# Top-k attention with a maxout MLP: one batch's scores kept in DRAM, the last batch in two halves, masks without sums

## The chip, the cores and the metric

The kernel runs on one core of one Trainium2 chip. The core has five engines with instruction queues of their own: PE (matrix products; PEld is its weight load), DVE (vector work on SBUF and PSUM), ACT (one function over a tile, with scale, bias and a sum), POOL (vector work on SBUF only) and SP (here it only issues DMAs). Each runs its queue in order and waits on semaphores for the others. The metric is the device time of one execution in microseconds (us).

## The reference

```python
def _attn_ref(q, k, v):                       # q, k, v: (8, 8, 576, 64) float32
    scores = scale * np.matmul(q, k.transpose(0, 1, 3, 2))
    kth = np.partition(scores, -32, axis=-1)[..., -32:-31]
    scores = np.where(scores >= kth, scores, -1000000000.0)
    scores = scores - np.max(scores, axis=-1, keepdims=True)
    attn = np.exp(scores)
    attn = attn / (np.sum(attn, axis=-1, keepdims=True) + 1e-09)
    return np.matmul(attn, v)

def _moe_ref(x, w1, w2, w3, w_out):           # x: (4608, 512), w: (512, 768), w_out: (768, 512)
    h = np.maximum(np.maximum(x @ w1, x @ w2), x @ w3)
    return h @ w_out
```

Attention keeps the 32 largest of 576 scores in each row. Its output, all heads side by side, goes through an MLP that takes the largest of three products.

## The kernel before

**Units.** A batch has 8 heads, taken as 4 pairs. A unit is (batch, pair, quarter): 128 queries against all 576 keys for both heads of a pair, so a score tile of 128 x 2 x 576. The last 64 queries of two pairs make one mixed unit. There are 18 units in a batch and 144 in all; `units` lists them, and its order is the order of ranks.

**A unit's steps.** `qk` makes the scores on PE. For the first batch (`whole`) and for all mixed units it takes the float32 inputs as they are, 4 or 8 matmuls; for the rest `prep` has cut queries and keys into a high and a low part (an ACT cast, a POOL subtraction), and 12 matmuls add three products. There is one PSUM tile for scores. `evac` (ACT) copies and scales them into one of five score tiles `ssb` in SBUF. `sweep` (DVE) takes the eight largest of each seventh of a row into `L`. `negate` (POOL) and `pivot` (DVE, five pieces p1 to p5) work out a pivot `Q[0]` that lies between the 24th and the 32nd largest: p1 takes the eight largest of the lower halves of `L`, p2 and p3 work on the negated upper halves, p4 joins them. `sign` (ACT) writes the sign of pivot minus score and sums it, which counts the scores above the pivot. `window` (POOL) multiplies scores and signs, `below` (DVE) takes the eight largest under the pivot, and `place`, `leave`, `pick` choose the 32nd by the count. `mask` (DVE) pushes the scores under it away and also sums how many they are. `expo` (ACT), `denominator`, `inverse`, `widen`, `turn` (PE transposes), `turned` (ACT), `values` (PE) and `scaled_x` end in the batch's attention output.

**MLP.** `mlp` runs a batch's MLP in float16 products of high and low parts, in two passes of 256 and 320 tokens (the first batch in three spans). It needs the attention output of all pairs for its tokens and the weights, which DVE decodes (`decode`) and ACT and PE cut into two halves (`cut`) in the first 200 us.

**Review.** `review` compares the counts of a batch's masks with the values kept in `Q` and `kth`. If a row was not settled, a flag starts a loop at the end that does all batches again in a plain way.

**Order.** Nothing is left to the hardware: `in_order` takes all steps as pieces with an engine, a cost, needs and rings of buffers, and writes the queues. Each engine takes the piece of lowest rank that can start soon enough; ranks are the unit's number plus an offset for the kind of step (`OFFSETS`). The MLP's pieces are in `fill`: PE takes them when nothing else can start. Queues run as written, so a late piece holds up all that stands behind it.

Of the kernel before, what the change touches and what calls it, by code (L numbers as in the profile page):

```python
# [27 lines left out]
FULL = 1  # L28
PMB = 2
# [3 lines left out]
STICK = 59.0  # L33
WINDOW = 150
LEAD = 69.6
LOCK_A = -150.0
LOCK_B = -100.0
OFFSETS = {'E0': -9.14, 'E1': -5.65, 'E2': 1.85, 'N': -40.3, 'T0': 2.84, 'T1': 9.84, 'T2': 3.75, 'Y': -2.73, 'Z':
# [33 lines left out]
def in_order(pieces, fill):  # L72
# [34 lines left out]
    left = len(pieces) + len(fill)  # L107
    while left:
        best = None
        low = min((q[0].rank for q in queues.values() if q), default=0.0)  # L110
# [12 lines left out]
        (fills if fills[x.engine][:1] == [x] else queues)[x.engine].remove(x)  # L123
# [1052 lines left out]
```

## Time and profile before

| | |
|---|---|
| median of 3 runs | 1194.25 us (1192.98 to 1196.03) |
| profiled execution, device time | 1193.76 us |
| its span | 1192.0 us |
| PE busy | 1132.5 us (95%) |
| DVE busy | 1098.2 us (92%) |
| ACT busy | 1023.2 us (86%) |
| POOL busy | 825.2 us (69%) |
| mean DMA traffic | 46 GB/s |

The span is the time from the first to the last instruction that the profiler saw. An engine is busy while an instruction of it runs; waiting, branching and issuing DMAs are not counted. PE's matmuls overlap in its pipeline and their ends are modelled, so the distance from one start to the next tells more of PE than a busy time.

### The profile page before, as it was taken

How to read it: one execution, taken by the hardware profiler on the slowest of the kernel's cores; microseconds unless marked ns; L12 is line 12 of the kernel's file. 1: busy time of each engine (PE TensorE's matmuls, PEld its weight loads, DVE VectorE, ACT ScalarE, POOL GpSimd, SP SyncE). 2: the span in 40 equal slices, each digit the busy share in tenths (PEclk: the TensorE clock that was granted, in tenths of full speed). 3: DMA queues.
4: the chain of work that ended last, by engine and by line, in shares of the span. 5: the costliest groups of instructions: out<-in, count | busy, mean ns of one | idle time of the engine just before them, and what ended most of it. 6: DMA issues, size and time to landing. Idle time of an engine off the chain costs nothing.

```text
span 1192.0 us, 30104 instructions
## 1 busy us (share of the span) xinstructions
PE 1132.5 (95%) x9699; PEld 814.3 (68%) x9699; DVE 1098.2 (92%) x5543; ACT 1023.2 (86%) x2390; POOL 825.2 (69%) x1277
## 2 busy tenths in 40 slices
PE   5668889999999999999999999999999999999997
PEld 2344557878777767676777768676777768676864
DVE  6999999999999999999999999999999999999611
ACT  3878999999989898999988989899999999899621
POOL 2454776778778867778777878777877877877410
PEclk8789989999999999999999999999999999999999
DMA  8521111001110022002110021002100021000000
GB/s 290 209 86 38 59 34 62 2 28 61 38 43 10 1 88 61 19 2 70 41 40 10 2 87 61 19 2 70 60 21 11 1 88 32 19 2 10 10 18 30
DMA packets 28677, 54.70 MB, mean 46 GB/s; under 512 B 7776, under 2 KB 7776, under 8 KB 28512
## 3 DMA queue, kind: packets, MB, share of 16 engines
q1 hardware_dynamic: 28512, 52.71, 13.3%
q8 instruction: 78, 1.28, 0.5%
q14 instruction: 87, 0.71, 0.2%
HBM read 43.25 MB, written 9.44 MB: 44 GB/s over the span
## 4 chain that ended last, share of the span: by engine, by line
PE 64%; DVE 24%; ACT 6%; POOL 3%; issue 2%; DMA 1%; SPq 0%; ACTq 0%; DVEq 0%; POOLq 0%
PE m L766 28%; PE tr L709 9%; PE tr L678 8%; PE s L511 7%; PE m L826 6%; DVE L L528 6%; DVE Q L581 5%; DVE ssb L622 5%; PE s L503 2%; ACT w L567 2%; POOL w L575 2%; ACT pm L632 1%; DVE h L775 1%; PE tr L673 1%; DVE nR L552 1%
## 5 line engine op out<-in xcount | busy, mean ns | idle before, releaser
L575 POOL TENSOR_TENSOR w<-ssb,w 128x576 f32<-128x576 f32 x288 | 407.2, 1422 | 145.2 <-ACT w L567 54.9
L766 PE MATMUL m<-xh,wall 128*128 128x256 f16 (+3 forms) x2448 | 439.0, 279 | 4.1 <-ACT wall L336 3.5
L766 PEld LDWEIGHTS <-wall 128*128 128x128 f16 x3672 | 347.6, 98 | 82.6 <-issue 13.3
L766 PE MATMUL m<-xl,wall 128*128 128x256 f16 (+3 forms) x1224 | 339.1, 279 | 0.0
L528 DVE MAX8 L<-ssb 128x8 f32<-128x82 f32 (+1 forms) x2016 | 315.8, 228 | 1.8 <-ACT ssb L519 1.7
L632 ACT ACTIVATE pm<-ssb,nb 128x576 f32<-128x576 f32 x288 | 224.2, 779 | 25.5 <-DVE ssb L622 20.6
L622 DVE SCALAR_TENSOR_TENSOR ssb<-ssb,kth 128x576 f32<-128x576 f32 x288 | 238.4, 839 | 0.2
L567 ACT ACTIVATE w<-ssb,Q 128x576 f32<-128x576 f32 x288 | 222.3, 775 | 14.0 <-DVE Q L560 12.9
L690 ACT COPY pT<-tr 128x512 f32<-128x512 f32 (+1 forms) x432 | 215.8, 512 | 20.7 <-PE tr L675 9.9
L581 DVE MAX8 Q<-w 128x8 f32<-128x576 f32 x288 | 215.9, 750 | 5.1 <-POOL w L575 4.3
L678 PE MATMUL tr<-ident,pm 128*128 128x128 f32 x1152 | 178.7, 281 | 12.8 <-ACT pm L632 9.1
L519 ACT ACTIVATE ssb<-s 128x1152 f32<-128x1152 f32 x144 | 163.6, 1136 | 20.3 <-PE s L503 18.9
L709 PE MATMUL tr<-pT,vt 128*64 128x256 f32 (+2 forms) x2000 | 177.6, 327 | 1.0 <-ACT pT L690 1.0
L678 PEld LDWEIGHTS tr<-ident,pm 128*128 128x128 f32 x1152 | 130.2, 142 | 54.8 <-ACT pm L632 20.3
L709 PEld LDWEIGHTS tr<-pT,vt 128*64 128x64 f32 x2000 | 111.2, 138 | 61.9 <-issue 21.5
L775 DVE SCALAR_TENSOR_TENSOR h<-m,rises,h 128x256 f32<-128x256 f32 (+3 forms) x204 | 99.8, 489 | 45.4 <-PE m L766 42.7
L826 PE MATMUL m<-wall,hh 128*128 128x512 f16 x432 | 128.6, 379 | 0.0
L781 POOL TENSOR_TENSOR hl<-h,hh 128x256 f16<-128x256 f32 (+3 forms) x102 | 83.2, 816 | 61.7 <-ACT hh L778 61.0
L511 PE MATMUL s<-kT,qT 64*128 64x288 f32 x1344 | 118.6, 308 | 0.9 <-ACT ssb L519 0.8
L511 PEld LDWEIGHTS s<-kT,qT 64*128 64x128 f32 x1344 | 92.3, 184 | 33.8 <-issue 12.8
L826 PE MATMUL m<-wall,hl 128*128 128x512 f16 x216 | 81.9, 379 | 0.0
L534 POOL TENSOR_SCALAR nA<-L 128x56 f32<-128x56 f32 x144 | 52.1, 361 | 38.5 <-DVE L L528 28.6
(116 smaller groups left out, 1503.7 us busy)
## 6 DMA issues: line engine op xcount, KB each, us to landing
raw<-in_k_dram SPq DMA_DIRECT2D x36, 288.0 KB, 3.5
raw<-in_q_dram SPq DMA_DIRECT2D x36, 288.0 KB, 3.6
vt<-in_v_dram SPq DMA_DIRECT2D x32, 256.0 KB, 3.9
out_dram<-ob SPq DMA_DIRECT2D x32, 256.0 KB, 2.0
wall<-in_moe_w_dram SPq DMA_DIRECT2D x8, 768.0 KB, 7.4
wall<-in_moe_w_out_dram SPq DMA_DIRECT2D x3, 512.0 KB, 10.0
vt<-in_v_dram SPq DMA_DIRECT2D x64, 16.0 KB, 3.5
xh<-in_moe_w_out_dram SPq DMA_DIRECT2D x2, 512.0 KB, 4.1
```

Of the source, the lines that this page charges most:

```text
L511: nc.tensor.matmul(s[:, h, i, :HALF], qT[sl, qa, u * P:(u + 1) * P], kT[sl, ka, i * HALF:(i + 1) * HALF], start=(n_ == 0), stop=(n_ == 2))
L528: nc.vector.max(d["L"][:, t, g, :], d["ssb"][t][:, g * S // G:(g + 1) * S // G])
L567: nc.scalar.activation(d["w"][t], d["ssb"][t], AF.Sign, bias=d["Q"][:, t, 0:1], scale=-1.0, accum_out=d["cnt"][:, t:t + 1])
L575: x = nc.gpsimd.tensor_tensor(d["w"][t], d["ssb"][t], d["w"][t], ALU.mult)
L581: nc.vector.max(d["Q"][:, t, 1:NW], d["w"][t])
L622: x = nc.vector.scalar_tensor_tensor(ss, ss, d["kth"][:, t:t + 1], ss, ALU.is_lt, ALU.subtract, accum_out=d["lost"][:, t:t + 1])
L632: nc.scalar.activation(d["pm"][:, t], d["ssb"][t], AF.Exp, bias=d["nb"][:, t:t + 1], scale=-1.0 / SHRINK, accum_out=d["sums"][:, t:t + 1])
L678: nc.tensor.transpose(pt[:, j * P:(j + 1) * P], pm[:, i, 64 * i + j * P:64 * i + (j + 1) * P], ident)
L690: nc.scalar.copy(pT[:, 512 * i:512 * i + m] if i < 2 else pT[:, 8 * P:10 * P], pt[:, :m])
L709: nc.tensor.matmul(xp[64 * h:64 * h + 64, to], vt[:, 4 * h + i if i < 4 else 8 + h, :], keys, start=(i == 0), stop=(i == 4))
L766: nc.tensor.matmul(box["ps", i][:, :c1 - c0], a, bb[:, kc, c0:c1], start=(kc == 0 and k == 0), stop=(kc == KC - 1 and k == 2))
L826: nc.tensor.matmul(box["po"][:n], a[:, f, cs], bb, start=(f == 0 and k == 0), stop=(f == FC - 1 and k == 2))
```

## The change

**Parking.** The scores of the second batch (`PARKED`: all its four pairs) are made early. `load_parked` loads a pair into a tile of the ring `kT`, `qk` makes whole float32 products (no `prep` for this batch), `park` (ACT) copies them into a tile of the ring `qT`, `put` stores that to DRAM. These three pieces, for 18 units, are in a third list, `sooner`: ACT takes them before anything else that can start, PE, DVE, POOL and SP after. `fetch` later brings a unit's scores from DRAM straight into one of the five `ssb` tiles, in the place of `evac`. The third batch's first cast waits for the last parked units, since it takes the same tiles.

**Last batch.** Its units are listed by halves: quarters 0 and 1 of all pairs, then quarters 2, 3 and the mixed unit of pairs 2 and 3, then those of pairs 0 and 1. Pairs 0 and 1 are loaded and cast twice.

**Masks.** `mask` gives no sum any more. The count comes from `sign` alone, whose scale is now one step under -1, with the pivot one step lower too (`BELOW`): a new POOL step `lower` scales the lower halves of `L` for each unit, and p1 waits for it. `review` checks the pivots, counts and distances instead.

**Order.** The offsets, the patience of each engine and two limits have new values. First-batch score products now wait for the mask of the unit five places before.

```diff
--- before.py
+++ after.py
@@ -21,30 +21,33 @@
+BELOW = 1.0 - 2.0 ** -24
+PARKED = ((1, 0), (1, 1), (1, 2), (1, 3))
...
-STICK = 59.0
+STICK = 8.0
...
-LEAD = 69.6
+LEAD = 70
...
-OFFSETS = {'E0': -9.14, 'E1': -5.65, 'E2': 1.85, 'N': -40.3, 'T0': 2.84, 'T1': 9.84, 'T2': 3.75, 'Y': -2.73, 'Z':
+OFFSETS = {'E0': -5.32, 'E1': -2.13, 'E2': 1.74, 'N': -39.99, 'T0': 0.89, 'T1': 12.13, 'T2': 12.74, 'Y': -4.59, 'Z':
...
+            some = spares[e][:1] + some if e == "ACT" else some + spares[e][:1]
...
+    def load_parked(b, hp):
+        raw = wk.tile([P, 2, S], F32R, name="kT").bitcast(F32).rearrange("p a s -> p (a s)")
+        nc.sync.dma_start(raw[:, S:], k[b, hp])
+        nc.sync.dma_start(raw[:, 0:S], q[b, hp])
+        qk_of[b, hp] = raw
+
+    dram = ctx.enter_context(tc.tile_pool(name="dram", bufs=1, space=bass.MemoryType.DRAM))
+
+    def is_parked(n):
+        b, hp, u = units[n]
+        return (b, hp) in PARKED
+
+    def park(n):
+        d = st[n]
+        t = wk.tile([P, 2, S], F32R, name="qT").bitcast(F32)
+        nc.scalar.activation(t.rearrange("p h (i n) -> p h i n", i=2), d.pop("s")[:, :, :, :HALF], AF.Copy, scale=SCALE)
+        d["t"] = t
+
+    def put(n):
+        d = st[n]
+        x = d["away"] = dram.tile([P, 2, S], F32, name=f"away{n}")
+        nc.sync.dma_start(x, d.pop("t"))
+
+    def fetch(n):
+        x = st[n]["away"]
+        open_unit(n)
+        d = st[n]
+        t = wk.tile([P, 2, S], F32, name="ssb", bufs=NSSB)
+        d["ssb"] = [t[:, 0], t[:, 1]]
+        nc.sync.dma_start(t, x)
...
-    def whole(b, u):
-
-        return u == NU or b < FULL
+    def whole(b, hp, u):
+
+        return u == NU or b < FULL or (b, hp) in PARKED
...
-    nc.gpsimd.iota(spots, pattern=[[2, NW]], base=S + 3 - 2 * TOPK, channel_multiplier=0, allow_small_or_imprecise_dtypes=True)
+    nc.gpsimd.iota(spots, pattern=[[2, NW]], base=S + 1 - 2 * TOPK, channel_multiplier=0, allow_small_or_imprecise_dtypes=True)
...
+    def lower(n):
+
+        b = st[n]["L"][:, :, :, 4:8]
+        nc.gpsimd.tensor_scalar(b, b, BELOW, 1.0, ALU.mult, ALU.mult)
...
-        nc.scalar.activation(d["w"][t], d["ssb"][t], AF.Sign, bias=d["Q"][:, t, 0:1], scale=-1.0, accum_out=d["cnt"][:, t:t + 1])
+        nc.scalar.activation(d["w"][t], d["ssb"][t], AF.Sign, bias=d["Q"][:, t, 0:1], scale=-BELOW, accum_out=d["cnt"][:, t:t + 1])
...
-        x = nc.vector.scalar_tensor_tensor(ss, ss, d["kth"][:, t:t + 1], ss, ALU.is_lt, ALU.subtract,
-                                           accum_out=d["lost"][:, t:t + 1])
+        x = nc.vector.scalar_tensor_tensor(ss, ss, d["kth"][:, t:t + 1], ss, ALU.is_lt, ALU.subtract)
...
-        Q, kth, lost = books.pop(b)
-        eq = wk.tile([P, DF], BF16, name="junk", bufs=2).bitcast(F32)[:, :NT * NW].rearrange("p (i j) -> p i j", j=NW)
-        nc.vector.tensor_tensor(eq, Q, kth.unsqueeze(2).to_broadcast((P, NT, NW)), ALU.is_equal)
-        same = sm.tile([P, NT], F32, name="same", bufs=1)
-        nc.vector.tensor_reduce(same, eq, AX.X, ALU.add)
+        Q, kth, cnt = books.pop(b)
+        off = sm.tile([P, 2, NT], F32, name="off", bufs=1)
+        nc.gpsimd.tensor_tensor(off[:, 0], kth, Q[:, :, 0], ALU.subtract)
+        nc.gpsimd.tensor_tensor(off[:, 1], Q[:, :, 1], kth, ALU.subtract)
         yield
-        over = sm.tile([P, NT], F32, name="over", bufs=1)
-        nc.gpsimd.tensor_tensor(over, lost, same, ALU.add)
-        yield
-        nc.vector.tensor_reduce(bad[:, 0, b:b + 1], lost, AX.X, ALU.max)
-        nc.vector.tensor_reduce(bad[:, 1, b:b + 1], over, AX.X, ALU.min, negate=True)
+        part = sm.tile([P, NT], I32, name="part", bufs=1)
+        nc.vector.tensor_scalar(part, Q[:, :, 0].bitcast(I32), 0x7FFFFF, None, ALU.bitwise_and)
+        nc.vector.tensor_reduce(bad[:, 0, b:b + 1], part, AX.X, ALU.max)
+        nc.vector.tensor_reduce(bad[:, 1, b:b + 1], kth, AX.X, ALU.min, negate=True)
+        nc.vector.tensor_reduce(bad[:, 2, b:b + 1], cnt, AX.X, ALU.max)
+        nc.vector.tensor_reduce(bad[:, 3, b:b + 1], cnt, AX.X, ALU.min, negate=True)
+        nc.vector.tensor_tensor(off[:, 0], off[:, 0], off[:, 1], ALU.min)
+        nc.vector.tensor_reduce(bad[:, 4, b:b + 1], off[:, 0], AX.X, ALU.max)
...
+    lb = B - 1
+    at_ = units.index((lb, 0, 0))
+    assert len(units) - at_ == 18
+    units[at_:] = [(lb, hp, u) for hp in range(NP) for u in (0, 1)] + [(lb, hp, u) for g in (2, 0) for hp, u in ((g, 2), (g, 3), (g, NU), (g + 1, 2), (g + 1, 3))]
...
+            x = Piece("PE", cost, lambda: qk(n), [raw_of_pair[b, hp + a][0] for a in mine], 0.0, [(rings["s"], rel)], mode)
+            for a in mine:
+                raw_of_pair[b, hp + a][1].append(x)
+            y = Piece("ACT", 1080, lambda: park(n), [x], 0.0, [(rings["stage"], put_)])
+            z = Piece("SP", 1900, lambda: put(n), [y])
+            rel.append(y)
+            put_.append(z)
+            sooner.extend([x, y, z])
+            p("e", "SP", 1900, lambda: fetch(n), needs=[z], takes=[("ssb", held(n, "ssb")), *takes[1:]])
...
-        p("p1", "DVE", 186, lambda: pivot(n, 1), needs=[d["s", 1]] + ([of[n - 3]["p4"]] if n >= 3 else []))
+        p("n", "POOL", 243, lambda: lower(n), needs=[d["s", 1]])
+        p("p1", "DVE", 186, lambda: pivot(n, 1), needs=[d["n"]] + ([of[n - 3]["p4"]] if n >= 3 else []))
...
+    for x in first_splits:
+        x.needs.extend(sooner[-6:])
...
```

**Where instructions stand now.** Three places, each as the queue has it. On PE, in the first batch, around the value products of its second pair, before (L503 are score products from a loaded pair `raw`, L673 to L678 transposes, L709 value products, L274 sums over decoded weights):

```order
L503 MATMUL s<-raw_111 128x288 x4
L673 MATMUL tr<-ident,pm 128x128
L675 MATMUL tr<-ident,rsw 128x128
L678 MATMUL tr<-ident,pm 128x128 x4
L709 MATMUL tr<-pT,vt_93 64x128 x10
```

and in the new order (L543 from `kT` are parked score products, L333 and L339 cut weights, L718 to L723 transposes, L754 value products):

```order
L723 MATMUL tr<-ident,pm 128x128 x4
L543 MATMUL s<-kT 128x288 x4
L333 MATMUL m<-wall,times_413 128x384
L718 MATMUL tr<-ident,pm 128x128
L720 MATMUL tr<-ident,rsw 128x128
L543 MATMUL s<-kT 128x288 x4
L339 LDWEIGHTS less
L339 MATMUL m<-wall,less 128x384
L543 MATMUL s<-raw_112 128x288 x4
L754 MATMUL tr<-pT,vt_93 64x128 x10
```

Two parked units stand between the first batch's own steps. Counted over the new order, 13 of the 18 parked units stand ahead of the transposes of the ninth unit and the other 5 between there and the nineteenth's. MLP matmuls ahead of the 17th unit's transposes were 228 and are 354; ahead of the 25th's, 483 and 465; behind the last value products, 396 and 366.

On POOL, in the third batch, before (L534 is the negation, L575 `window`, L588 to L594 `place` and `leave`, L638 `denominator`, L737 the low part of the attention output):

```order
L534 TENSOR_SCALAR nA<-L 128x56
L575 TENSOR_TENSOR w<-ssb,w 128x576
L588 TENSOR_TENSOR oh<-spots,cnt 128x18
L590 TENSOR_SCALAR oh<-oh 128x18
L638 TENSOR_SCALAR den<-sums 128x2
L737 TENSOR_TENSOR xl<-xs,xh 128x256
L594 TENSOR_TENSOR oh<-oh,Q 128x18
```

and in the new order, in the same batch (L574 the negation, L579 the new step `lower`, L619 `window`, L632 to L638 `place` and `leave`, L681 `denominator`, L782 the low part):

```order
L574 TENSOR_SCALAR nA<-L 128x56
L619 TENSOR_TENSOR w<-ssb,w 128x576
L681 TENSOR_SCALAR den<-sums 128x2
L782 TENSOR_TENSOR xl<-xs,xh 128x256
L632 TENSOR_TENSOR oh<-spots,cnt 128x18
L634 TENSOR_SCALAR oh<-oh 128x18
L638 TENSOR_TENSOR oh<-oh,Q 128x18
L579 TENSOR_SCALAR L<-L 128x14x4
```

The new step need not follow the negation: here six other steps of POOL stand between the two. On SP, the first fetches stand between the last stores of parked scores: a fetch waits there for a free score tile, and the next store is the row behind it.

## Rows read from the trace of the kernel before

**Rows 1.** Busy times of the whole span, then PE, PEld, DVE, ACT, POOL by stretch.
```profile
PE 1132.5 (95%) x9699; PEld 814.3 (68%) x9699; DVE 1098.2 (92%) x5543; ACT 1023.2 (86%) x2390; POOL 825.2 (69%) x1277
...
0.00:200.00 200.00, 149.59 (x1150) 97.03 (x1151) 184.27 (x879) 156.34 (x357) 103.66 (x181) 0.89 0.33 113
200.00:1112.00 912.00, 908.90 (x7992) 665.88 (x7990) 894.31 (x4617) 844.98 (x1985) 708.11 (x1076) 1.00 0.10 34
```

**Rows 2.** Timeline of PE, two score units: start, length, instruction.
```profile
286.01 1.20 PE L503 MATMUL s<-raw 64*64 64x288 f32 x16
287.14 0.34 PE L766 MATMUL m<-xh,wall 128*128 128x192 f16 x2
...
597.71 1.05 PE L511 MATMUL s<-kT,qT 64*128 64x288 f32 x12
598.69 0.33 PE L673 MATMUL tr<-ident,pm 128*128 128x128 f32 x1
```

**Rows 3.** Timeline of DVE and PE, the last mask and the last value products.
```profile
1117.13 0.81 DVE L622 SCALAR_TENSOR_TENSOR ssb<-ssb,kth 128x576 f32<-128x576 f32 x1
...
1125.83 1.39 PE L709 MATMUL tr<-pT,vt 128*64 128x64 f32 x40
...
1127.21 2.07 PE m L766 x18
```

**Rows 4.** Timeline of PE, two whole float32 score units of the first batch.
```profile
47.84 2.16 PE L503 MATMUL s<-raw 64*128 64x288 f32 x8
...
60.08 1.24 PE L503 MATMUL s<-raw 64*128 64x288 f32 x8
```

**Rows 5.** Groups of PE instructions from 200 to 1112 us, score products of cut inputs.
```profile
L511 PE MATMUL s<-kT,qT 64*128 64x288 f32 x1296 | 114.4, 308 | 0.1
```

**Rows 6.** Groups of instructions, the evacuation: busy us, mean ns, idle before.
```profile
L519 ACT ACTIVATE ssb<-s 128x1152 f32<-128x1152 f32 x144 | 163.6, 1136 | 20.3 <-PE s L503 18.9 <-PE s L511 0.3
```

**Rows 7.** Busy times from 120 to 200 us, columns as in rows 1.
```profile
120.00:200.00 80.00, 68.85 (x681) 48.74 (x680) 77.16 (x389) 75.82 (x180) 54.89 (x90) 0.95 0.16 49
```

**Rows 8.** DMA issues: KB each, median us to landing.
```profile
raw<-in_k_dram SPq DMA_DIRECT2D x36, 288.0 KB, 3.5
```

**Rows 9.** Timeline of DVE and POOL, two stretches in mid-kernel.
```profile
431.54 0.75 DVE L581 MAX8 Q<-w 128x8 f32<-128x576 f32 x1
...
432.21 0.80 DVE L622 SCALAR_TENSOR_TENSOR ssb<-ssb,kth 128x576 f32<-128x576 f32 x1
432.48 0.58 POOL L638 TENSOR_SCALAR den<-sums 128x2 f32<-128x2 f32 x1
...
432.94 0.81 DVE L622 SCALAR_TENSOR_TENSOR ssb<-ssb,kth 128x576 f32<-128x576 f32 x1
...
435.27 0.67 POOL L737 TENSOR_TENSOR xl<-xs,xh 128x256 f16<-128x256 f32 x1 [1.16 <-ACT xh L733]
...
435.33 0.65 DVE L557 SCALAR_TENSOR_TENSOR z<-n,b 128x18 f32<-128x18 f32 x1
...
602.06 0.24 POOL L534 TENSOR_SCALAR nA<-L 128x56 f32<-128x56 f32 x1
```

**Rows 10.** Groups of instructions: the negation, masks, sum readings, review.
```profile
L622 DVE SCALAR_TENSOR_TENSOR ssb<-ssb,kth 128x576 f32<-128x576 f32 x288 | 238.4, 839 | 0.2
...
L534 POOL TENSOR_SCALAR nA<-L 128x56 f32<-128x56 f32 x144 | 52.1, 361 | 38.5 <-DVE L L528 28.6 <-DVE kth L599 7.3 <-DVE z L557 1.0
...
L622 DVE DVE_READ_ACCUMULATOR ssb<-ssb,kth 128x1 f32 x288 | 22.9, 79 | 0.0
...
L655 DVE TENSOR_TENSOR junk<-Q,kth 128x324 f32<-128x324 f32 x8 | 5.2, 644 | 0.0
...
L657 DVE TENSOR_REDUCE same<-junk 128x36 f32<-128x324 f32 x8 | 3.9, 491 | 0.3
...
L663 DVE TENSOR_REDUCE bad<-over 128x1 f32<-128x36 f32 x8 | 1.5, 182 | 0.2
```

**Rows 11.** Busy time of the masks' line in the first 200 us (count behind it).
```profile
0.00:200.00 200.00, 31.50 (x76) 0.89 0.33 113
```

More of the change, by code (lines that the diff above doesn't have):

```diff
@@ L69, in __init__, with in_order @@
         self.size, self.users = size, []
-def in_order(pieces, fill):
-    queues, fills = {e: [] for e in LATE}, {e: [] for e in LATE}
+def in_order(pieces, fill, sooner):
+    queues, fills, spares = ({e: [] for e in LATE} for _ in range(3))
     for x in sorted(pieces, key=lambda x: x.rank):
@@ L80, in in_order @@
         fills[x.engine].append(x)
+    for x in sooner:
+        spares[x.engine].append(x)
     free = {e: 0.0 for e in LATE}
@@ L105, in ready @@
         return t
-    left = len(pieces) + len(fill)
+    left = len(pieces) + len(fill) + len(sooner)
     while left:
@@ L122, in in_order @@
         t, x = best
-        (fills if fills[x.engine][:1] == [x] else queues)[x.engine].remove(x)
+        next(z for z in (fills, spares, queues) if z is queues or z[x.engine][:1] == [x])[x.engine].remove(x)
         x.start = t
@@ L133, in in_order @@
         left -= 1
-PATIENCE = {'PE': 114, 'DVE': 133, 'ACT': 31, 'POOL': 37, 'SP': 0}
+PATIENCE = {'PE': 124, 'DVE': 97, 'ACT': 82, 'POOL': 45, 'SP': 0}
 @with_exitstack
@@ L904, in p @@
             turn_ = [of[n - 1][key]] if takes and n and key in of[n - 1] else []
-            x = piece(engine, cost, run, [*needs, *turn_], n, takes, mode, alone, key if isinstance(key, str) else key[0] + str(key[1]))
+            x = piece(engine, cost, run, [*needs, *turn_], n, takes, mode, alone,
+                      "pe" if key == "e" and engine == "SP" else key if isinstance(key, str) else key[0] + str(key[1]))
             d.setdefault(key, x)
@@ L913, in attention @@
             takes.append(("books", opened[b]))
-        p("q", "PE", 1000 if whole(b, u) else 806, lambda: qk(n), needs=[x for k in preps_of[n] for x in (loaded if whole(b, u) else prepared)[k]],
-          takes=takes, mode="rows" if full else "quarters")
-        p("e", "ACT", 1080, lambda: evac(n), needs=[d["q"]], takes=[("ssb", held(n, "ssb"))])
-        rel.append(d["e"])
+        cost, mode = 1000 if whole(b, hp, u) else 806, "rows" if full else "quarters"
+        if is_parked(n):
+            q_, put_ = [], []
+            for a in mine:
+                if (b, hp + a) not in raw_of_pair:
+                    last = list(raw_of_pair.values())[-1:]
+                    used = []
+                    raw_of_pair[b, hp + a] = piece("SP", 1900, lambda a=a: load_parked(b, hp + a), [x for x, _ in last], 2.0 * len(raw_of_pair),
+                                                   [("raw", used)], tag="pl"), used
+            x = Piece("PE", cost, lambda: qk(n), [raw_of_pair[b, hp + a][0] for a in mine], 0.0, [(rings["s"], rel)], mode)
+            for a in mine:
+                raw_of_pair[b, hp + a][1].append(x)
[5 more added lines that the diff above has]
+            p("e", "SP", 1900, lambda: fetch(n), needs=[z], takes=[("ssb", held(n, "ssb")), *takes[1:]])
+        else:
+            p("q", "PE", cost, lambda: qk(n), needs=[*(x for k in preps_of[n] for x in (loaded if whole(b, hp, u) else prepared)[k]),
+                                                     *([of[n - NSSB]["m", 0]] if b == 0 and n >= NSSB else [])], takes=takes, mode=mode)
+            p("e", "ACT", 1080, lambda: evac(n), needs=[d["q"]], takes=[("ssb", held(n, "ssb"))])
+            rel.append(d["e"])
         for i in range(2):
@@ L940, in attention @@
         for t in range(2):
-            p(("m", t), "DVE", 790, lambda t=t: mask(n, t), needs=[d["h"]], alone=True)
+            p(("m", t), "DVE", 715, lambda t=t: mask(n, t), needs=[d["h"]], alone=True)
             p(("x", t), "ACT", 770, lambda t=t: expo(n, t), needs=[d["m", t], d["p2"]] + ([d["x", 0]] if t else []),
@@ L1049 @@
         prepare(pi)
+    for b in range(B):
+        if b not in scaled_v:
+            values_of(b)
     weights()
@@ L1053 @@
         for p_ in preps_of[n_]:
-            for x in raw_users[p_] if whole(*units[n_][::2]) else users[p_]:
+            for x in raw_users[p_] if whole(*units[n_]) else users[p_]:
                 x.needs.append(of[n_]["q"])
+    for x in first_splits:
+        x.needs.extend(sooner[-6:])
     for b in range(B):
@@ L1076 @@
     with tc.manual_schedule():
[L1077 to L1083 removed]
+        in_order(pieces, fill, sooner)
+    limits = const.tile([P, 5], F32, name="limits")
+    for i, most_ in enumerate((2.0 ** 23 - 1.5, -LEAST, S - 2.0 * (TOPK - 8) + 0.5, 2.0 * TOPK - S + 0.5, -2.0 ** -125)):
+        nc.vector.memset(limits[:, i:i + 1], most_)
+    worst = sm.tile([P, 5], F32, name="worst")
     nc.vector.tensor_reduce(worst, bad, AX.X, ALU.max)
```

44 lines of the change are left out of this document (22 added, 22 removed), and 18 rows, old and new, of the table OFFSETS.

## The prediction

> **What bounds the kernel now.** I read the busy times first, for the whole span and by stretch [rows 1]. In the first 200 us PE, the matrix engine, is busy for 149.6 us and idle for 50.4, while DVE is busy for 184.3. From 200 to 1112 us PE is busy for 908.9 of 912 us and DVE for 894.3; of DVE's 1098.2 us only 20 are left after that, and PE runs the last matmuls of the MLP. A busy PE need not be at its peak, so the second view was the timeline of PE [rows 2]: a score unit's 12 matmuls start at 597.71 us and the next matmul at 598.69, with no hole behind them. From 200 us on the end is PE's: work taken out of that stretch shortens the run by its own length as long as DVE keeps up. The start is not PE's but DVE's, which is decoding weights and searching the first tiles.
>
> DVE is the second bound, close behind. Its last mask starts at 1117.13 us, and the last value products, which wait for it through ACT and PE, start at 1125.83 [rows 3], 8.7 us later. From there to the end at 1192.0 there are 66.2 us of PE. So the forecast needs two accounts, one for PE and one for DVE; the later of the two is the end.
>
> **The change part by part.**
>
> *Scores of the second batch.* Its 16 full units leave their old places on PE, 0.98 us each (597.71 to 598.69), and so do its two mixed units, 1.13 us each (286.01 to 287.14) [rows 2]: 16 x 0.98 + 2 x 1.13 = 17.9 us. They come back as whole float32 products in the start. Such a product took 2.16 us in one place there and 1.24 in another [rows 4] (the granted clock averages 0.89 in that stretch [rows 1]), so 18 of them cost between 22 and 39 us of PE. Its 50.4 idle us hold either. If that cover were gone, all 22 would come back and nothing would be won. By the new order 13 of the 18 stand ahead of the ninth unit's transposes and the other 5 between there and the nineteenth's. In the old order a few of these products stood before 200 us, where PE had gaps: 1296 of the 1344 matmuls of this kind lie behind it [rows 5], so four full units lie before. At worst only 12 full units and the mixed ones count, 14.0 us. I take 17.9, because the new order has 354 MLP matmuls ahead of the 17th unit's transposes where there were 228, so there is work to close those gaps.
>
> *Its evacuations.* 18 ACT copies of 1.136 us [rows 6] move as well, 20.4 us. ACT is idle for 43.7 us of the first 200 [rows 1], but only for 4.2 of the 80 from 120 us on [rows 7]. The 5 late ones need 5.7 us there, and the casts of this batch's queries and keys fall away, most of them in and soon after that stretch. I take nothing, with 20.4 us as the upper end. In the last batch two pairs are loaded and cast a second time; these four casts fall where ACT has room.
>
> *The way out and back.* 18 stores and 18 loads of 576 KB go through SP's one queue. No row has this size; a load of 288 KB lands after 3.5 us [rows 8], so a fetch takes between 3.5 us and twice that, against the 1.136 us of the evacuation that it replaces. In between stand five score tiles, and a unit takes DVE 1098/144 = 7.6 us, so a fetch has a lead of several units if SP is free. I take nothing. If SP is late, each trip round the five tiles loses the difference of 2.4 to 5.9 us, with 18/5 trips at most 21 us on DVE's account. What stands behind a waiting fetch on SP is the next store, and behind that ACT's next parking copy.
>
> *Masks without sums.* A mask starts at 432.21 and the next one at 432.94, 0.73 us; the search over the same 576 elements starts at 431.54 and is followed at 432.21, 0.67 us [rows 9]. The difference, 0.06 to 0.07 us, is about the 79 ns of reading the sum [rows 10]. With 0.07 x 288 masks DVE gives back 20.2 us. The bounds are 0 (the first search may be the shorter for another reason) and 288 x 0.079 = 22.8. Of this, 38 masks lie before 200 us (76 instructions, half of them readings [rows 11]) and bring the end of the start forward, by 2.7 us. The rest only helps DVE's account.
>
> *The review.* Per batch a product of 644 ns, a sum of 491 and two small ones of about 182 go, 1.50 us; seven small ones of 182 come, 1.27 [rows 10]: 8 x 0.23 = 1.8 us less on DVE.
>
> *One more POOL step for each unit.* 144 instructions like the negation, 0.24 us alone [rows 9] and 0.361 in the mean [rows 10], so 35 to 52 us on an engine that is idle for 367 [rows 1]. It stands ahead of the DVE step that takes the eight largest of the lower halves. I take nothing, since DVE has other units' work between, and leave its price to a rival.
>
> *Last batch by halves, order refitted.* In the old order 396 MLP matmuls stand behind the last value products, in the new 366: 30 fewer, 18 of which take 2.07 us [rows 3], so 3.4 us move ahead of that point. PE does them anyway: nothing on PE's account.
>
> The sum: 1192.0 - 17.9 - 2.7 = 1171.4 us of span, and 1.8 us lie around the span (1193.76 less 1192.0): 1173 us. The profiled execution stands 0.5 us under the median, which I leave out.
>
> DVE's account: 1117.1 - 20.2 - 1.8 = 1095.1 for the last mask, + 8.7 to the last value products, + 66.2 - 3.4 = 1166.6 of span, 1168 us. It ends 5 us ahead of PE's.
>
> **The rivals.**
>
> *DVE's account decides.* If PE closes more of its gaps than I take, the end comes at 1168, and with 22.8 us for the masks at 1166. For it: 126 more MLP matmuls early. Against: by the 25th unit the order has 465 of them against 483, so it gives the lead back.
>
> *The start grows.* The parked copies stand first in ACT's queue, and one PSUM tile serves all score products, so a parked unit can hold up a unit that DVE waits for. If the whole 20.4 us land on DVE's path, the end is 1173 + 20 = 1193, no change; with half of it, 1183. For it: ACT is busy for 75.8 and DVE for 77.2 of the 80 us from 120 us on [rows 7]. Against: most parked units come before that.
>
> *POOL takes it back, and the run is slower.* The mechanism is the new POOL step in DVE's path. The rows show that the two engines hold each other up: a POOL step of two columns took 0.58 us beside a mask, and DVE's small two-input step took 0.65 us when it began 0.06 us after a POOL subtraction of 0.67 [rows 9]. If DVE stands once for every new step, for its 0.24 us alone, DVE's account grows by 144 x 0.24 = 34.6 us: 1168 + 34.6 = 1203; with 0.361 it is 1220. It makes the run slower from (1193.8 - 1168.4)/144 = 0.18 us a unit on. Against: the negation stands in the same place between POOL and DVE, and DVE is busy for 894 of 912 us. The Trainium skill, on the page "SBUF — State Buffer" in the section "SBUF: two separate sides", says that a DVE instruction with two SBUF inputs and a POOL instruction need one shared port pair under an exclusive lock, which the first of them holds for its whole length. By that rule the new step blocks a mask whenever it starts first, which is this rival; the 0.65 us agree with it, but a mean of 839 ns for all masks beside 0.80 for the one in the row says that POOL's present steps seldom hit them.
>
> *The repeat runs.* The count now rests on what ACT's sign gives for the pivot itself. If that came out otherwise, the review would start the unplanned loop over all batches: 144 units x 2 x 4 searches of 0.75 us are 864 us on DVE alone, so over 2050 us. Nothing in the trace speaks for it.
>
> **How the numbers follow.** Forecast 0.59, DVE decides 0.14, the start grows 0.15, POOL 0.10, the repeat 0.02. A measurement of this kernel can tell 0.3%, 3.6 us, from no change. The forecast and DVE's account are faster, and so is the part of the third case under 1190, 0.08; its other 0.07 are no change; the last two cases are slower. So faster 0.81, same 0.07, slower 0.12. The range goes from 1160 (DVE's account with the upper price for the masks, less five of the slow score products at their fast length, 5 x 0.92 = 4.6 us) to 1190, where the third case stops being faster.
>
> **What would show it.** Right: PE idle for under 35 us of the first 200, the 18 parked products there, masks under 0.68 us apart, and PE without holes behind 200 us. For POOL: DVE idle in front of the step on the lower halves, or masks with a mean above 839 ns. For the start: the last parked copy behind 210 us and DVE idle for over 25 us before it. The forecast is wrong if DVE's last mask comes after 1105 us, or if PE's work behind 200 us has not become shorter by about 18 us.

## The result, and the profile after

The changed kernel took 1201.26 us (median of 5 runs, 1200.68 to 1204.66), the kernel before 1194.31 beside it: a ratio of 1.0058, 95% interval 1.0043 to 1.0073. It is slower by 6.9 us, where 21 us faster was forecast, and the time lies outside the range. The profiled execution has a span of 1202.9 us, 10.9 longer than before. It is the slowest of the five (1204.66 us), so a difference that is read from the two traces can be up to 4 us larger than the 6.9 of the medians.

The busy times of the whole span, then the chain of waits by engine, both from the profile of the changed kernel, and last the same chain of the kernel before:

```profile
PE 1140.0 (95%) x9635; PEld 806.6 (67%) x9635; DVE 1107.9 (92%) x5282; ACT 1020.9 (85%) x2386; POOL 873.5 (73%) x1425
...
DVE 33%; PE 27%; POOL 9%; ACT 6%; issue 3%; DMA 0%; SPq 0%; POOLq 0%; ACTq 0%; DVEq 0%
...
PE 64%; DVE 24%; ACT 6%; POOL 3%; issue 2%; DMA 1%; SPq 0%; ACTq 0%; DVEq 0%; POOLq 0%
```

Against [rows 1] DVE has 9.7 us more, where the forecast took some 22 away, and POOL 48 more. In the chain (the work that ended last, followed back from the end) PE had the larger share before and DVE has it now. The busy times by stretch (PE, PEld, DVE, ACT, POOL, then the granted clock), and three pieces of 20 us:

```profile
0.00:200.00 200.00, 164.31 (x1339) 110.32 (x1340) 184.14 (x863) 164.95 (x370) 109.81 (x205) 0.97 0.54 188
200.00:1112.00 912.00, 891.59 (x7661) 638.34 (x7659) 893.01 (x4342) 824.18 (x1943) 738.76 (x1184) 1.00 0.13 42
...
200.00:220.00 20.00, 16.99 (x127) 11.16 (x124) 19.70 (x104) 16.70 (x43) 13.62 (x24) 1.00 0.35 119
220.00:240.00 20.00, 15.72 (x95) 9.00 (x95) 19.62 (x101) 18.78 (x47) 13.25 (x25) 1.00 0.27 90
320.00:340.00 20.00, 18.53 (x195) 13.76 (x193) 19.31 (x94) 15.59 (x38) 13.76 (x27) 1.00 0.27 85
```

PE's busy time from 200 to 1112 us went from 908.9 to 891.6, the 17 us that were to go. But they came back as idle time: 20.4 us, where there were 3.1. In the first of the three pieces PE is idle for 3.0 us and DVE for 0.3. DVE is as full as it was. The timelines of DVE and PE at the end:

```profile
1126.64 1.80 DVE L666 SCALAR_TENSOR_TENSOR ssb<-ssb,kth 128x576 f32<-128x576 f32 x1
1129.80 1.95 DVE L666 SCALAR_TENSOR_TENSOR ssb<-ssb,kth 128x576 f32<-128x576 f32 x2
...
1138.67 2.38 PE L754 MATMUL tr<-pT,vt 128*64 128x256 f32 x20
```

DVE's last two masks end at 1131.75, the last value products start at 1138.67 (1125.83 in [rows 3]), and 64.2 us follow (66.2 before). So the attention is 12.8 us later and the tail 2 us shorter. The groups of masks, of the small two-input step z, and of the new POOL step (busy us, mean ns):

```profile
L666 DVE SCALAR_TENSOR_TENSOR ssb<-ssb,kth 128x576 f32<-128x576 f32 x288 | 248.3, 874 | 0.3
L579 POOL TENSOR_SCALAR L<-L 128x56 f32<-128x56 f32 x144 | 48.6, 337 | 10.9
L602 DVE SCALAR_TENSOR_TENSOR z<-n,b 128x18 f32<-128x18 f32 x144 | 39.9, 277 | 0.0
L587 DVE MAX8 b<-L 128x8 f32<-128x28 f32 x288 | 38.3, 174 | 0.4
```

The mean of a mask rose from 839 ns [rows 10] to 874. DVE hardly waits for the new step (0.4 us in front of L587, the step that takes its result): it is held up inside its instructions and, as shown below, in front of steps that wait for POOL's other results.

### The profile page after: what moved, and what is told of

It reads as the page before. It is cut to its first block, busy times and chain, and to the rows that moved or that the text cites. A ratio compares the mean times of both kernels' runs of the same rounds, so it can differ in the third digit from the quotient of the medians.

```text
span 1202.9 us, 29880 instructions
## 1 busy us (share of the span) xinstructions
PE 1140.0 (95%) x9635; PEld 806.6 (67%) x9635; DVE 1107.9 (92%) x5282; ACT 1020.9 (85%) x2386; POOL 873.5 (73%) x1425
## 4 chain that ended last, share of the span: by engine, by line
DVE 33%; PE 27%; POOL 9%; ACT 6%; issue 3%; DMA 0%; SPq 0%; POOLq 0%; ACTq 0%; DVEq 0%
PE m L811 13%; DVE L L568 9%; DVE ssb L666 7%; DVE Q L625 6%; POOL w L619 4%; PE m L871 4%; PE tr L723 3%; PE tr L754 3%; PE s L551 3%; DVE h L820 3%; ACT w L611 2%; DVE nR L597 1%; ACT pT L735 1%; DVE z L602 1%; DVE xs L764 1%
## 5 line engine op out<-in xcount | busy, mean ns | idle before, releaser
L619 POOL TENSOR_TENSOR w<-ssb,w 128x576 f32<-128x576 f32 x288 | 407.2, 1419 | 104.0 <-ACT w L611 48.8
L666 DVE SCALAR_TENSOR_TENSOR ssb<-ssb,kth 128x576 f32<-128x576 f32 x288 | 248.3, 874 | 0.3
L735 ACT COPY pT<-tr 128x512 f32<-128x512 f32 (+1 forms) x432 | 212.4, 512 | 11.9 <-PE tr L720 6.7
L723 PE MATMUL tr<-ident,pm 128*128 128x128 f32 x1152 | 177.3, 281 | 18.2 <-DVE xs L764 8.1
L754 PE MATMUL tr<-pT,vt 128*64 128x256 f32 (+2 forms) x2000 | 175.5, 325 | 0.0
L723 PEld LDWEIGHTS tr<-ident,pm 128*128 128x128 f32 x1152 | 128.1, 141 | 68.2 <-issue 24.9
L559 ACT ACTIVATE ssb<-s 128x1152 f32<-128x1152 f32 x126 | 142.7, 1133 | 11.8 <-PE s L543 10.6
L754 PEld LDWEIGHTS tr<-pT,vt 128*64 128x64 f32 x2000 | 109.4, 137 | 59.4 <-issue 16.6
L551 PE MATMUL s<-kT,qT 64*128 64x288 f32 x1152 | 101.7, 308 | 1.0 <-ACT ssb L559 1.0
L551 PEld LDWEIGHTS s<-kT,qT 64*128 64x128 f32 x1152 | 79.2, 184 | 28.8 <-ACT ssb L559 9.9
L681 POOL TENSOR_SCALAR den<-sums 128x2 f32<-128x2 f32 x144 | 46.1, 320 | 45.9 <-ACT pm L675 36.5
```

Of the source, the lines that this page charges most:

```text
L551: nc.tensor.matmul(s[:, h, i, :HALF], qT[sl, qa, u * P:(u + 1) * P], kT[sl, ka, i * HALF:(i + 1) * HALF], start=(n_ == 0), stop=(n_ == 2))
L619: x = nc.gpsimd.tensor_tensor(d["w"][t], d["ssb"][t], d["w"][t], ALU.mult)
L666: x = nc.vector.scalar_tensor_tensor(ss, ss, d["kth"][:, t:t + 1], ss, ALU.is_lt, ALU.subtract)
L723: nc.tensor.transpose(pt[:, j * P:(j + 1) * P], pm[:, i, 64 * i + j * P:64 * i + (j + 1) * P], ident)
L735: nc.scalar.copy(pT[:, 512 * i:512 * i + m] if i < 2 else pT[:, 8 * P:10 * P], pt[:, :m])
L754: nc.tensor.matmul(xp[64 * h:64 * h + 64, to], vt[:, 4 * h + i if i < 4 else 8 + h, :], keys, start=(i == 0), stop=(i == 4))
```

## The experiments

All ratios are to the kernel before, run beside it; "us" is 1194.3 x (ratio - 1).

| run | edit | ratio, 95% interval | us |
|---|---|---|---|
| e1 | before, scores of cut inputs by 4 of 12 matmuls | 0.9918 (0.9901 to 0.9935) | -9.8 |
| e2 | before, masks on 432 columns | 0.9928 (0.9903 to 0.9953) | -8.6 |
| e5 | before, both | 0.9729 (0.9710 to 0.9749) | -32.4 |
| e13 | before, e1 for the second batch only | 1.0000 (0.9984 to 1.0015) | 0.0 |
| e14 | before, second batch's scores by DMA | 1.0009 (0.9993 to 1.0024) | +1.1 |
| e3 | before, masks without sums | 0.9986 (0.9974 to 0.9998) | -1.7 |
| e4 | before, with the new POOL step | 1.0061 (1.0047 to 1.0075) | +7.3 |
| e15 | the same, nothing waits for it | 1.0049 (1.0032 to 1.0066) | +5.9 |
| e6 | after, without that step | 1.0004 (0.9990 to 1.0018) | +0.5 |
| e17 | after, that step on ACT | 1.0047 (1.0028 to 1.0066) | +5.6 |
| e16 | after, masks on 432 columns | 0.9913 (0.9891 to 0.9935) | -10.4 |
| e7 | after, nothing parked (new plan) | 1.0186 (1.0173 to 1.0200) | +22.2 |
| e8 | after, count of before (new plan) | 1.0073 (1.0058 to 1.0087) | +8.7 |
| e9 | after, mask cost 790 (new plan) | 1.0161 (1.0142 to 1.0179) | +19.2 |
| e10 | after, old table (new plan) | 1.0299 (1.0276 to 1.0322) | +35.7 |
| e11 | after, no halves (new plan) | 1.0100 (1.0085 to 1.0114) | +11.9 |
| e12 | before, parking alone (new plan) | 1.0180 (1.0159 to 1.0202) | +21.5 |

**Is the end PE's?** e1 and e2 relieve one engine each, e5 both, in the order of before:

```
-            for n_, (qa, ka) in enumerate(((0, 0), (0, 1), (1, 0))):     # e1
+            for n_, (qa, ka) in enumerate(((0, 0),)):
-        ss = d["ssb"][t]                                                 # e2 (mask)
+        ss = d["ssb"][t][:, :432]
```

> The kernel before, in its own order, with only the first of the three partial products of every cut score unit (4 matmuls for 12; scores of lower precision). That takes 864 matmuls of 0.98/12 us = 71 us off PE, nearly all behind 200 us, and nothing off any other engine. Theory A of the forecast (the end is PE's behind 200 us): 1194 - 71 = about 1123 us, until DVE decides at about 1185. Theory B (DVE's chain of searches and masks sets the pace, and PE looked full only because its queue had MLP work to fill in): DVE has the same work, so over 1180 us, and PE gets idle by 60 us or more.

> The kernel before, in its own order, with every mask on 432 of 576 columns (the other quarter stays unmasked): about 0.17 us less on DVE for each of 288 masks, 0.17 x 288 = 49 us, nothing less on PE. Theory A (PE's end): only the start gets shorter, 38 masks x 0.17 = 6 us, so about 1188 us. Theory B (DVE sets the pace): 25 to 45 us less, 1150 to 1170 us, unless PE, with 3 us idle behind 200 us, cannot follow; then about 1185.

> The kernel before, in its own order, with both cuts at once: one of three partial products in the cut score units (71 us off PE) and masks on 432 of 576 columns (43 us off DVE by the busy time of that run). Alone they gave 9.5 and 9.1 us. Theory B' (PE and DVE are both within about 10 us of the end, so either alone holds it): together far more than the sum, DVE's last mask at 1117 - 43 = about 1075 and 75 us behind it, 1140 to 1160 us. Rival D (something else, ACT with 845 busy of 912 us or the waits between the engines, sets the pace at about 1185): no more than the sum, 1175 to 1185 us.

From 200 to 1112 us, of e1, e2 and e5 in this order, and a score unit of e1 on PE's timeline:

```profile
200.00:1112.00 912.00, 880.33 (x7231) 613.83 (x7226) 900.06 (x4640) 848.27 (x2006) 714.71 (x1087) 1.00 0.10 34
...
595.04 0.52 PE L511 MATMUL s<-kT,qT 64*128 64x288 f32 x4
595.50 0.33 PE L673 MATMUL tr<-ident,pm 128*128 128x128 f32 x1
```

```profile
200.00:1112.00 912.00, 909.14 (x8001) 668.02 (x8000) 867.25 (x4601) 845.84 (x1987) 683.60 (x1077) 1.00 0.10 33
...
DVE h L775 <- PE m L766: 19.9, 49, 0.9
```

```profile
200.00:1112.00 912.00, 894.51 (x7373) 628.15 (x7374) 868.01 (x4618) 845.29 (x2004) 687.66 (x1084) 1.00 0.10 33
```

A unit of 4 matmuls takes 0.46 us, not a third of 0.98, so e1 takes 112 x 0.52 = 58 us off PE and not 71. It gained 9.8: PE then stands idle for 31.7 us while DVE is busy for 900 of 912. e2 made the masks 43 us shorter in sum; DVE's busy time fell by 34 us (1064.7 for 1098.2) and the run by 8.6: now PE is full (909) and DVE waits for it, 19.9 us (49 times) in front of the MLP's maximum alone. Both at once gained 32.4, far more than 9.8 + 8.6, though less than my 1140 to 1160 us. So neither A nor B as first put is right: in this order PE and DVE each hold the end, and relieving one of them by 58 or by 34 us brings no more than 10.

**Parking's share of PE's work, in a fixed order.** e13 makes e1's edit for batch 1 only; e14 drops matmuls and evacuation for that batch:

```
+        if b == 1:                       # in qk: no matmuls; in evac: a DMA of 576 KB in place of the copy
+            nc.sync.dma_start(t, q[b, hp // 2 * 2:hp // 2 * 2 + 2].rearrange("a p s -> p a s"))
```

> The kernel before, in its own order, with the first of three partial products alone in the second batch's 16 full units: 128 matmuls of 0.082 us, 10.5 us off PE between 200 and 350 us, nothing else. The forecast's step (an end held by PE shortens by its own length): 1184 us. Theory B' (DVE holds the end there; with all units cut, the first 72 masks came 0.8 us sooner): 1192 to 1195 us, PE idle for about 10 us more behind 200 us.

> The kernel before, in its own order, with the second batch's scores neither computed nor evacuated: 576 KB of the input's numbers come by DMA in place of each of the 18 units (these are not its scores). That is what parking gives at most, without its cost in the start: 17.9 us off PE and 20.4 off ACT. The forecast's step: 1176 us. Theory B' (DVE holds the end): 1188 to 1194 us, PE idle for 15 us or more behind 200 us.

```profile
200.00:1112.00 912.00, 898.23 (x7819) 656.05 (x7814) 891.83 (x4614) 830.61 (x1967) 705.59 (x1074) 1.00 0.13 43
```

The row is e14's: PE idle for 13.8 us, and no gain. e13 took 16 x 0.52 = 8.3 us off PE (not 10.5) and gained nothing within 1.9 us. The 9.8 us that e1 gained over 112 units would be 1.4 for these 16, so a gain that small is not excluded. The forecast's -17.9 is a gain of 2 us at most in this kernel and its order, even without parking's cost in the start.

**The same work seen from the other side.** e16 makes e2's edit in the changed kernel:

> The changed kernel, in its own order, with masks on 432 of 576 columns (the other quarter stays unmasked): about 43 us off DVE, nothing off PE. In the kernel before this gave 9 us, and PE held the rest. Theory B' (the change did take PE's 18 us away, and only DVE hides it): about twice as much, PE's 21 idle us behind 200 us go and the start gets 4 us shorter, 1176 to 1184 us. Rival H (parked scores gave PE nothing in the end): no more than before, 1191 to 1195 us.

```profile
200.00:1112.00 912.00, 902.99 (x7825) 654.00 (x7823) 874.59 (x4370) 834.67 (x1978) 725.07 (x1206) 1.00 0.13 40
```

1183.67 us. Against the changed kernel that is 10.4 + 6.9 = 17.3 us, twice the 8.6 of e2. So PE's 18 us were taken away and lie hidden behind DVE. PE's idle time fell to 9.0 us, not to 3. The two are not quite alike: e16 took 39 us off DVE's busy time (1068.8 for 1107.9), 5 more than e2.

**The sum of the masks.**

```
-        x = nc.vector.scalar_tensor_tensor(ss, ss, d["kth"][:, t:t + 1], ss, ALU.is_lt, ALU.subtract,
-                                           accum_out=d["lost"][:, t:t + 1])
+        x = nc.vector.scalar_tensor_tensor(ss, ss, d["kth"][:, t:t + 1], ss, ALU.is_lt, ALU.subtract)
```

> The kernel before, in its own order, with the sum left out of the masks alone (the count of what was masked is not taken). The forecast's step: 0.07 x 288 = 20 us less on DVE, starts of masks 0.07 us closer, 2.7 us of it in the start on PE's account: 1191 us, or down to 1175 where DVE sets the pace. Theory B2 (the reading of the sum runs beside the end of the mask): mask to mask only 0.01 us closer, 3 us on DVE, 1191 to 1194 us.

```profile
431.66 1.54 DVE L622 SCALAR_TENSOR_TENSOR ssb<-ssb,kth 128x576 f32<-128x576 f32 x2
433.13 0.15 DVE L641 RECIPROCAL rs<-den 128x2 f32<-128x2 f32 x1
...
L622 DVE SCALAR_TENSOR_TENSOR ssb<-ssb,kth 128x576 f32<-128x576 f32 x288 | 237.7, 838 | 0.2
```

The same two masks as in [rows 9], now without sums: 1.54 us from the first one's start to the second one's end. With sums they began at 432.21 and 432.94 and the second took 0.81: 1.54 us too. The next step follows 1.47 us after the first start here, which is 0.73 us a mask, the distance in [rows 9]. The 79 ns of reading ran beside the mask's end. DVE's busy time fell by 1.9 us in all (1096.4 for 1098.2) and the run by 1.7, as theory B2 has it.

**The new POOL step.** e4 puts it into the kernel before, e15 lets it write to a tile that nobody reads, e6 takes it out of the changed kernel, e17 gives it to ACT there:

```
+        b = d["L"][:, :, :, 4:8]                                          # e4, in negate; e15: into a scratch tile
+        nc.gpsimd.tensor_scalar(b, b, 1.0, 1.0, ALU.mult, ALU.mult)
-        nc.gpsimd.tensor_scalar(b, b, BELOW, 1.0, ALU.mult, ALU.mult)     # e6: left out
+        nc.scalar.activation(b, b, AF.Copy, scale=BELOW)                  # e17
```

> The kernel before, in its own order, with one more POOL step behind each negation, on the lower halves of the eight largest (a product with 1, so no value changes), and DVE's step on these waits for it, as after the change. The forecast: nothing, 1194 us. Theory C (DVE's two-input instructions wait for POOL's port): masks and the small two-input step get longer, together 15 us on DVE, 1200 to 1212 us; the mean of a mask goes from 839 ns to 870 or more.

> The kernel before, in its own order, with the same extra POOL step behind each negation, written to a scratch tile that nobody reads, so that no DVE step waits for it. With the wait this was 1203 us. Theory C (POOL's port, and POOL being later with its other steps): still 1200 to 1204 us. Rival W (DVE's wait for the step's end is the cost): 1194 to 1197 us.

> The changed kernel, in its own order, with the new POOL step on the lower halves left out (the pivot can then be a score itself, and the count off by one there). Theory C (this step costs DVE 0.065 us a unit by its port, as in the kernel before with it, 7.5 us): 1192 to 1196 us, masks with a mean nearer 840 ns. Rival E (the parked scores or the new order cost the time, and the step comes for nothing, as forecast): 1199 to 1202 us.

> The changed kernel, in its own order, with the new step on the lower halves done by ACT in place of POOL, at the same place of the program; DVE's step on them waits for it as before. Theory C (the price is POOL's time and port): as without the step, 1194 to 1198 us, POOL's busy time back near 825 us, unless ACT, which is idle for 180 of 1203 us and gets some 35 more, holds up the signs behind it. Rival W' (a wait for another engine between the sweep and the step on the lower halves is the price, whoever does it): 1201 to 1206 us.

Groups of e4, then of e6, then of e17, with the wait that e17 adds (us, times, longest):

```profile
L624 DVE SCALAR_TENSOR_TENSOR ssb<-ssb,kth 128x576 f32<-128x576 f32 x288 | 241.3, 848 | 0.2
L536 POOL TENSOR_SCALAR L<-L 128x56 f32<-128x56 f32 x144 | 55.7, 387 | 0.2
```

```profile
L665 DVE SCALAR_TENSOR_TENSOR ssb<-ssb,kth 128x576 f32<-128x576 f32 x288 | 244.2, 860 | 0.3
L601 DVE SCALAR_TENSOR_TENSOR z<-n,b 128x18 f32<-128x18 f32 x144 | 39.8, 276 | 0.0
```

```profile
L666 DVE SCALAR_TENSOR_TENSOR ssb<-ssb,kth 128x576 f32<-128x576 f32 x288 | 243.6, 858 | 0.3
L579 ACT ACTIVATE L<-L 128x56 f32<-128x56 f32 x144 | 36.2, 252 | 4.8 <-DVE L L568 4.8
...
DVE b L587 <- ACT L L579: 5.1, 13, 1.0
```

In the kernel before, this step alone costs 7.3 us, as much as the whole change. In the changed one, taking it out gives back 6.9 - 0.5 = 6.4. Most of it stays when nothing waits for the step (5.9), so it is mostly POOL's time and not the step's result that DVE pays for. The masks got longer, but in e4 by 9 ns and not by the 31 that I expected, 2.9 us in all; in the changed kernel, against e6, by 14 ns, 4.1 us. The new step hardly blocks them itself: counted over the trace of the changed kernel, the 17 masks that begin while it runs take 808 ns in the mean and none over 817. Longer are those that begin behind `window` or another long POOL step (`window` lengthened 39 masks, 25 in e6); that these come later because POOL has one step more for each unit is argued. Another part stands in front of the DVE steps that wait for POOL's other results, `pick` (kth) and `inverse` (rs), here before and in e15:

```profile
L599 DVE TENSOR_REDUCE kth<-oh 128x2 f32<-128x18 f32 x144 | 22.8, 159 | 1.4 <-POOL oh L594 0.6
L642 DVE RECIPROCAL rs<-den 128x2 f32<-128x2 f32 x144 | 22.3, 155 | 3.3 <-POOL den L638 1.9
...
L601 DVE TENSOR_REDUCE kth<-oh 128x2 f32<-128x18 f32 x144 | 23.0, 160 | 3.1 <-POOL oh L596 1.6
L644 DVE RECIPROCAL rs<-den 128x2 f32<-128x2 f32 x144 | 22.6, 157 | 4.9 <-POOL den L640 3.0
```

DVE's idle time in front of the two grew by 1.7 and 1.6 us, most of it ended by `leave` (oh) and `denominator` (den). In the changed kernel the idle time in front of `below`, which waits for `window`, is 7.8 us with the step and 5.6 without (e6). How the price divides among these was not tested apart. On ACT the step leaves DVE's masks as they are without it (858 ns), but now DVE waits 5.1 us for ACT, and the time is that of the changed kernel within its interval: the price changed its form. Neither theory named for e17 holds alone.

**New plans.** e7 to e12 each change one part and let the planner write the order anew:

> The changed kernel with no batch parked: the second batch's scores are computed in their places, by 12 matmuls a unit, and the order is planned again by the same table of offsets. The forecast's step: the 17.9 us come back, 1219 us. Theory B' (PE stands idle for 20 us behind 200 us since DVE sets the pace): within 5 us of the changed kernel, 1197 to 1206 us, with PE idle for under 8 us there.

> The changed kernel with the count of the kernel before (sums on the masks, pivot and sign as before, no POOL step on the lower halves, the old review), mask cost 790 in the planner, and everything else as changed: parked scores, halves, the new table. The forecast's step: parking alone, 1194 - 17.9 = 1176 us. Theory B': DVE's work is that of the kernel before and sets the end, 1187 to 1197 us.

> The changed kernel, planned again with a mask cost of 790 as before the change and not 715 (the kernel without the sum showed 838 ns a mask, as with it). Theory F (the planner, told masks that are 75 ns too short, sets POOL's steps beside them and PE's filling too thin, and this is what is left of the loss besides the new POOL step): 1194 to 1199 us, masks with a mean nearer 840 ns. Rival G (the cost matters little, a new order only moves the collisions about): 1199 to 1208 us.

> The changed kernel, planned again with the table of offsets, the patience, the stick and the lead of before (the three new keys kept). The forecast put the refitted order at nothing: 1195 to 1207 us. Theory F' (the refitted table itself brings POOL's steps beside DVE's two-input steps; with the old one the small two-input step is back at 236 ns from 277 and masks nearer 840): 1190 to 1198 us. If the old table does not fit the new work: over 1210 us.

> The changed kernel with the last batch's units in the order of before (not by halves of its queries), planned again. The forecast: the halves move 30 MLP matmuls, 3.4 us, ahead of the last value products, and while DVE sets the end these come back: 1202 to 1207 us, with about 30 more MLP matmuls behind the last value products. Rival: halves cost something, 1195 to 1200 us.

> The kernel before with the parked second batch alone: masks with sums, pivot, sign, review, order of units, table of offsets and mask cost of before. The forecast's step: 17.9 us, 1177 us. Theory B' (DVE's work is that of before, 1084 us to the last mask with 34 us idle there, so DVE holds the end): PE idle for 12 to 25 us behind 200 us, last mask at 1110 to 1120 us, 1185 to 1197 us.

These tell little of the parts. Their edits are `PARKED = ()`; the old count with cost 790; `790` for `715`; the old OFFSETS, PATIENCE, STICK and LEAD; the last line on `units` left out; parking with all else as before. The times run from 1205 to 1231 us, though by the forecast's step only e7's edit was to cost more than 6 us over the changed kernel. e8, e9 and e12 lie above every range that was named for them; e10 lies where the old table does not fit the new work. e11 lies in the forecast's band, with 72 more MLP matmuls behind the last value products and not 30. e7 met the forecast's 1219 us, but not its reason: PE has 17.9 us more work there and still stands idle for 22.8 us from 200 us on:

```profile
200.00:1112.00 912.00, 889.23 (x7701) 638.25 (x7699) 884.33 (x4284) 829.84 (x1937) 743.04 (x1174) 1.00 0.11 34
```

And e12 adds the same parking to before and is 21.5 us slower. The table of offsets that was fitted to the old steps costs 29 us with the new ones (e10 against the changed kernel), more than any single edit in a fixed order; what halves and refit are worth stays open. No version that does all of the work was faster than the kernel before; the faster ones leave out products, a quarter of the masks or (e3, 1.7 us) the count.

## Why the prediction was wrong

**The step that failed first** is "From 200 us on the end is PE's: work taken out of that stretch shortens the run by its own length as long as DVE keeps up". Its condition decided, and DVE did not keep up. I had seen that DVE was busy for 894.3 of 912 us, but took the 66 us of MLP behind the last value products for something that would only move with PE. They start when the attention chain ends, and that ends when DVE does. PE looked full because its queue had MLP matmuls to fill in; less score work gave idle time (20.4 us) and not an earlier end (e13, e14: nothing).

**The term that let DVE look early** is "With 0.07 x 288 masks DVE gives back 20.2 us". It measured 1.7 us (e3), near the lower bound of 0. I took the gap after the search in [rows 9] for the proper length and the reading for the difference; without the reading the gap between masks stayed as it was. Without these 20.2 us, DVE's account by its own steps ends at 1168 + 20 = 1188, behind PE's 1173, and the forecast would have been a small gain.

**The new POOL step, "0":** 6.4 to 7.3 us (e6, e4). The reason given, that DVE has other units' work between, is true (DVE waits 0.4 us there) and beside the point. The rival with POOL had the sign, the engine and nearly the time (1203), but not the mechanism: DVE does not stand for 0.24 us a unit, and it is not the new step that blocks the masks but POOL's longer ones; it loses 6.4/144 = 0.044, and that decides only because the masks gave nothing. That its time came so near is luck.

**The review, "1.8 us less on DVE":** the seven new steps are not of 182 ns. Two take 542 and 371, the rest 180 to 191, 1.84 us for the 1.50 that went: 2.7 us more in 8 batches.

```profile
L702 DVE TENSOR_SCALAR part<-Q 128x36 int32<-128x36 int32 x8 | 4.3, 542 | 0.0
L707 DVE TENSOR_TENSOR off<-off 128x36 f32<-128x36 f32 x8 | 3.0, 371 | 0.0
```

**The order, "0":** in e6, with the new step gone, masks still have a mean of 860 ns and z of 276, where e3 has 838 for masks and [rows 10] 839. That is 6 us on the masks, and z adds 144 x (276 - 236) ns = 5.8. The group of z before, then timelines of DVE and POOL in the changed kernel:

```profile
L557 DVE SCALAR_TENSOR_TENSOR z<-n,b 128x18 f32<-128x18 f32 x144 | 34.0, 236 | 0.1
```

```profile
691.92 1.37 DVE L602 SCALAR_TENSOR_TENSOR z<-n,b 128x18 f32<-128x18 f32 x1
693.21 0.83 DVE L666 SCALAR_TENSOR_TENSOR ssb<-ssb,kth 128x576 f32<-128x576 f32 x1
...
681.37 0.16 DVE L602 SCALAR_TENSOR_TENSOR z<-n,b 128x18 f32<-128x18 f32 x1
681.44 2.00 DVE L666 SCALAR_TENSOR_TENSOR ssb<-ssb,kth 128x576 f32<-128x576 f32 x1
```

```profile
691.83 1.42 POOL L619 TENSOR_TENSOR w<-ssb,w 128x576 f32<-128x576 f32 x1 [0.85 <-DVE e L180]
...
681.36 1.46 POOL L501 TENSOR_TENSOR qT<-raw,qT 128x576 fp32r<-128x576 f32 x1 [0.28 <-ACT qT L498]
```

At 681.37 z took 0.16 us; it began within 0.01 us of a POOL subtraction. At 691.92 it began 0.09 us after a POOL window and ended 0.04 after it, 1.37 us later; the mask at 681.44 began 0.08 us after the subtraction and took 2.00. Counted over the whole trace of the changed kernel, the 78 masks that begin while POOL runs nothing take 0.81 us in the mean and none over 0.86. There are 50 that begin 0.03 us or more behind the start of a POOL step which has over 0.25 us still to go, 34 before; every one of these 84 ends 0.61 to 0.62 us after that step. From 0.81 and 0.62 I estimate that a POOL step with under 0.19 us to go costs a mask nothing, and the short new step mostly stays under that. The Trainium skill, page "SBUF — State Buffer", section "SBUF: two separate sides", says that a DVE step with two SBUF inputs and a POOL step that reads SBUF share a port pair, and that the one which starts first locks the other out for its whole length. The trace agrees for the long POOL steps, and shows no such lock for what is left of a short one. Neither the parking nor the new table is needed for these meetings: e7 parks nothing and has masks of 862 ns and z of 284, e10 has the old table and 866 and 268. What in the new steps or orders brings them was not shown apart.

**What held:** all 18 parked copies lie in the first 200 us, their 160 matmuls cost 23.3 us of PE (22 to 39 forecast), fetches land after 3.8 us and no unit waits for one, and the tail got 2.0 us shorter (3.4 forecast). The start did not grow: the last parked copy begins at 197.8 us, and DVE is idle for 15.9 of the first 200 us, 15.7 before. Of the signs of being right, PE's idle time in the start just missed (35.7 us, under 35 was the test), masks stayed 0.73 us from the next step (median) and PE has holes behind 200 us. The test that was to show a failure, a last mask after 1105 us, came true at 1130.

So the sum as measured: POOL's step +6.4; all else together +0.5 (e6). Taken one by one, the sums (-1.7), parking (0), the shorter tail (-2.0), the review (+2.7) and the meetings on the port (+11.8) would come to about 11 us, so some 10 us were won back by something that no run shows apart. Part of it may be DVE's idle time in front of the MLP's maximum, 45.4 us before and 42.1 in e6. Nor was parking's worth in the new order measured by itself.

## What to carry to other kernels

A full engine is the bound only if the work behind its last wait could start earlier: before counting a saving on one engine, run the kernel with a good part of that engine's work left out in the same order; here 58 us off PE gave 10. Where two engines are both nearly full, price an edit on each of them and believe only what both allow. Compare parts of a change in a fixed order, since a new plan moved the changed kernel by up to 29 us.

## What the runs showed of the hardware

- The reading of a DVE sum (79 ns, 288 times) adds next to nothing from one mask's start to the next one's: 0.73 us with it and without, and 1.9 us of DVE's busy time over all 288.
- A DVE step with two SBUF inputs of 18 columns took 1.37 us in place of 0.16 when POOL's 1.42 us product had begun 0.09 us earlier. Each of the 50 masks that began behind a POOL step with over 0.25 us to go ended 0.61 to 0.62 us after it; the 78 beside an idle POOL took 0.81 us.
- 144 POOL steps of 56 columns that nobody waits for made the run 5.9 us longer, 41 ns each, and DVE busy for 6.7 us more, though POOL was busy for only 872 of the 1200 us.
- Four matmuls of 288 columns took 0.46 us where twelve took 0.98, so leaving out two thirds of this group saved about half of its time.
